# A zero-padded last token tile in the low-rank sums, and six small attention groups moved behind the second layer of an older batch's small group

## The chip, the cores and the metric

The kernel runs on one core of a Trainium2 chip. The metric is device time in microseconds (us) of one execution. PE is TensorE, DVE is VectorE, ACT is ScalarE, POOL is GpSimd, and SP is SyncE, which issues all the transfers of this kernel.

## The reference

There are eight batches of 3136 tokens with 256 features. A gated attention is followed by a mixer with a low-rank sum over tokens and a two-layer network over features:

```
attn = maximum(z @ z.T / 3136, 0) ** 2      # z is 3136 x 64
x    = u * (attn @ v)                       # u, v are 3136 x 256
u2   = x + ((x.T @ U) @ V).T                # U is 3136 x 32, V is 32 x 3136
out  = u2 + maximum(u2 @ w_ch1, 0) @ w_ch2  # 256 -> 1024 -> 256
```

Inputs and output are float32; the matmuls work on bf16 copies.

## The kernel before, in words

The tokens of a batch are 25 tiles of 128 rows: 24 full ones and a last one with 64 rows (TAIL). Four full tiles make a group, so a batch has six groups of 512 tokens (g = 0 to 5) and a small group of 64 tokens (g = 6, called NQ). An item is one group of one batch; the kernel walks through 56 items (b, g), in order, and at each item it mixes work of three stages: the attention of (b, g); u2 of the group one batch earlier; and the two layers of the network (ch1 and ch2) for the group one batch and one item earlier. In item (b, 0) the last of these is the small group of batch b-2.

The order on every engine is written by the program itself. A planner keeps a clock in units of 256 matmul columns, an estimate of when ACT, DVE and SP come free (`book`, L109), and when each of the four PSUM buffers comes free (`ps_free`, `take_ps`). `emit` (L971) walks through a list of light units, which are pairs of matmuls of the attention sum or of ch2, and slips other work in at given places; an entry of such a queue is (place, PSUM buffers that must be free, urgent or not, function), and a place that needs buffers waits up to 14 units for them. Work for ACT and DVE that is not due yet is put into `held`. Each engine then does its instructions in that order.

Most matmuls are pairs: each operand is split into two halves of 64 rows, and the two halves are run side by side in tile shape 64*128 (rows * columns of TensorE). Both halves add into the same PSUM banks at different times; where they change banks, `post` (L164) puts a no-op on POOL that waits for the last matmuls on the old banks, and the next matmul waits for that no-op (recorded at L168 in the profile). A stream such as `ch2_stream` (L908) goes through all its units with one crossing of halves and banks, calls `post`, and then through all of them with the other: two passes of 16 pairs.

The names that the change and the steps of the prediction touch:

- `load_u` (L291) loads u of a group. All groups share the tile u_sb with two buffers.
- `score_small` makes the scores of the small group, one item before the batch begins. `last_turn` has the DMA transpose them for the full groups.
- `av_small` (L654) multiplies them with v: 50 matmuls of shape 64*64, whose four partial sums are added by `four_sums` (an ACT copy at L680, DVE adds at L682 and L684) and multiplied with u at L672. It runs in item (b, 6), the last of its batch, as `small` (L1289). Where that item has a ch2 stream, it is put at half of it, between the two passes: `qm += [(nC // 2, -1, False, small)]`. Items 6 and 55, the first and the last of these, have no such stream.
- `t1_all` (L737) makes the low-rank sum over all tokens of a batch at place 8 of the next batch's item 0: 24 matmuls of shape 128*32 and one of 64*32, for the last tile.
- `u2_unit` (L768) makes u2 of a group, casts it and has the DMA transpose it to u2T (`x_turn`, L730) for ch1. The first group's is marked as urgent; its ch1 begins at place 4 of item (b, 1).
- `ch2_small` (L951) is the second layer of a small group: 16 matmuls of shape 64*64 and `four_sums`. It runs in item (b, 0) of the second batch after its own: `qc.append((72, 1, False, lambda: ch2_small(*fin)))`.
- `issue_turn` (L371) has the DMA transpose a block of scores into the mirrored one (L384), or part of a diagonal block (L376).

All transfers stand in one queue on SP, in the order in which the program issues them; one that waits holds those behind it.

Of the kernel before, what the change touches and what calls it, by code (L numbers as in the profile page):

```python
# [8 lines left out]
FP32 = mybir.dt.float32  # L9
BF16 = mybir.dt.bfloat16  # L10
# [8 lines left out]
def kernel(  # L19
# [11 lines left out]
    nc = tc.nc  # L31

    B, S, D = u.shape
# [3 lines left out]
    P = 128  # L37
    NT = (S + P - 1) // P
    NF = S // P
# [4 lines left out]
    GT = 4  # L44
# [245 lines left out]

    def load_u(b, g):  # L291
        g0, gw = groups[g]
        t = pool.tile([P, GT, D], FP32, name="u_sb", bufs=2)
        if gw >= P:
            nc.sync.dma_start(
                out=t[:, : gw // P, :],
                in_=rows_of(u[b])[:, g0 // P : (g0 + gw) // P, :],
            )
        else:
            nc.sync.dma_start(out=t[:gw, 0, :], in_=u[b, g0 : g0 + gw, :])  # L300
        queued(gw)
        u_sbs[b, g] = t
# [292 lines left out]
    def av_stream(b, g, box):  # L595
        def lhs(h, q, jt):
            jb, j = divmod(jt, GT)
            while (b, jb) not in v_cast:
                if spare and not b:
                    spare.pop(0)()  # L600
                else:
                    run_held(min(h[0] for h in held))
            while (b, g, jb) not in blocks:
                if (g, jb, b) in ready_turns:
                    issue_turn((g, jb, b))
                else:
                    run_held(min(h[0] for h in held))
            t = blocks[b, g, jb][1]
            if jb >= g or made_twice(b, g, jb):
                while squared.get((b, g, jb), 0) < 2:  # L610
                    run_held(min(h[0] for h in held))
                if split(b, g, jb):
                    while j >= 2 and q < 2 and (b, g) not in split_turned:
                        if (g, g, b) in ready_turns:
                            issue_turn((g, g, b))
                        else:
                            run_held(min(h[0] for h in held))
                    x = in_split(j, q)
                    return t.rearrange("p a c -> p (a c)")[h, x : x + P]
                return t[h, j, q * P : (q + 1) * P]  # L620

            return t.rearrange("p a c -> p (a c)")[h, (q * GT + j) * P : (q * GT + j + 1) * P]

        per = 2 * GT

        def step(i, way, first, least):
            if first:
                xs[b, g] = pool.tile([P, GT, D], BF16, name="x_bf", bufs=8)
                box["k"], box["ps"] = take_ps()
            jt, a = divmod(i, 2)  # L630
            pair(
                box["k"],
                crossed(
                    way,
                    a,
                    lambda h, q: dict(
                        out=four(box["ps"])[:, q, :],
                        lhsT=lhs(h, q, jt),
                        rhs=v_bfs[b][h, jt, :],
                        start=first,  # L640
                        stop=False,
                    ),
                ),
                D,
            )
            while box.get("given", 0) < least // per:
                give_block(blocks[b, g, box.get("given", 0)])
                box["given"] = box.get("given", 0) + 1

        return Ways(2 * NF, 1, step, box)  # L650

    def av_small(b, g):  # L654
        k, ps = take_ps()
        rows = groups[g][1]
        xs[b, g] = pool.tile([P, GT, D], BF16, name="x_bf", bufs=8)
        for jt in range(NT):
            c = jt % 2
            for h in range(2):  # L660
                nc.tensor.matmul(  # L661
                    out=ps[c * hp : c * hp + rows, h, :D],
                    lhsT=smalls[b][h * hp : (h + 1) * hp, place_of(jt), :],
                    rhs=v_bfs[b][h * hp : (h + 1) * hp, jt, :],
                    start=(jt < 2),
                    stop=(jt >= NT - 2),
                    tile_position=(h * hp, c * hp),
                )
        pe(NT / 2 + 2)
        u1 = u_sbs[b, g]  # L670
        four_sums(k, ps, u1[:rows, 1:3, :])
        nc.vector.tensor_tensor(  # L672
            out=xs[b, g][:rows, 0, :], in0=u1[:rows, 1, :], in1=u1[:rows, 0, :], op=ALU.mult
        )
        book("dve", clock[0] + 3, 3)
# [61 lines left out]
    def t1_all(b):  # L737
        k, pt = take_ps()
        for g in range(NG):
            for q, it, rows in tiles_of(g):  # L740
                c = it % NREP
                nc.tensor.matmul(  # L742
                    out=pt[c * R : (c + 1) * R, 0, :D],
                    lhsT=U_bf[:rows, it, :],
                    rhs=xs[b, g][:rows, q, :],
                    start=(it < NREP),
                    stop=(it + NREP >= NT),
                    tile_position=(0, c * R),
                )
        pe(8)  # L750

        up = pool.tile([P, D], FP32, name="t1_up", bufs=1)
        t1 = pool.tile([P, D], BF16, name="t1_sb")
        nc.scalar.copy(out=up[:hp, :], in_=pt[hp:, 0, :D])
        nc.vector.tensor_tensor(out=t1[:hp, :], in0=pt[:hp, 0, :D], in1=up[:hp, :], op=ALU.add)
        nc.vector.tensor_copy(out=t1[hp:, :], in_=t1[:hp, :])
        book("act", clock[0] + 3, 5)
        ps_free[k] = book("dve", clock[0] + 10, 6)
        t1s[b] = t1
# [270 lines left out]
    def load_U():  # L1030
        entry, raw = stage_block()
        nc.sync.dma_start(out=raw[:, : NF * R].rearrange("p (t r) -> p t r", r=R), in_=rows_of(moe_U))
        nc.sync.dma_start(out=raw[:TAIL, NF * R : NT * R], in_=moe_U[NF * P :, :])
        queued(NF * R / 2)

        def casts():
            cast(U_bf[:, :NF, :], raw[:, : NF * R].rearrange("p (t r) -> p t r", r=R), NF * R)
            cast(U_bf[:TAIL, NF, :], raw[:TAIL, NF * R : NT * R], 100)
            give_block(entry)

        return [casts]
# [158 lines left out]
        todo[t] = todo[t][:most]  # L1200

    direct = (B - 1, 0)
    for t in range(n_items):
        slot[0] = t
        att = items[t]
# [4 lines left out]
        g_now = t % NG  # L1210
        b_next = t // NG + 1

        if t + 1 < n_items and t > NG:
            load_u(*items[t + 1])
        if t == n_items - 3:
            xTs[direct] = take_block()[1][:, : GT // 2, :].rearrange("p a (q d c) -> p (a q) d c", d=ND, c=P)
            x_turn(*direct, xTs[direct])
# [46 lines left out]
        if av and full:  # L1264

            last = nA - 9
            for h, x, y in zip(hs, (4, 22, 36, 62), (16, 32, 48, last)):
                qc.append((x, 1, False, one(h, 0)))
                qc.append((y, 0 if y == 32 else 1, y != 32, lambda h=h, y=y: (scores(y != 32), one(h, 1)())))
            n = len(mine) - 3  # L1270
            qs += [(9 + 74 * i / n, 1, False, lambda: scores(1)) for i in range(n)]
        elif av:

            for h, x in zip(hs, (22, 32, 42, 52)):
                qc += [(x, 1, False, one(h, 0)), (x + 8, 0, False, one(h, 1))]
            if fin:
                qc.append((72, 1, False, lambda: ch2_small(*fin)))
            k = min(2, len(mine) // 3)
            n = len(mine) - 3 * k
            at = [1 + 80 * i / n for i in range(n)]  # L1280
            if t == 0:
                at = [8, 8, 26, 38, 42, 56, 64, 72, 80]
                for i, x in ((2, 22), (3, 34)):
                    qm.append((x, 0, False, lambda i=i: z_turn(0, i * 2 * GT, on_act)))
            qs += [(x, 1, False, lambda: scores(1)) for x in at]
            qs += [(x, k, True, lambda: scores(k)) for x in (16, 48 if t else 46, nA - 2) if k]
        else:

            small = lambda: av_small(*att)  # L1289
            order = mine[:1] + [small] + mine[1:]  # L1290
            if mix:
                c0, c1, d0, d1, c2, c3, d2, d3 = parts(mix, box1)
                up = [lambda: u2_unit(*u2i)]
                if fin:
                    order = [c0] + mine[:1] + [c1, d0, d1] + [c2] + mine[1:] + [c3, d2, d3] + up
                else:
                    order = up + [small, c0, c1, d0, d1, c2, c3, lambda: t1_all(att[0]), d2, d3]
            qc += [(0, 0, False, f) for f in order]
# [79 lines left out]
```

## Time and profile before

| what | value |
|---|---|
| median of 3 runs | 992.4 us (991.75 to 994.2) |
| the profiled execution | 994.29 us, with a span of 992.5 us |
| PE, weight loads, DVE, ACT, POOL busy | 98%, 79%, 62%, 50%, 2% |
| granted TensorE clock | 1.00 |
| DMA | 176.4 MB, queue q1 86.8% of 16 engines' span |
| start of one small attention group to the next, batches 1 to 6 | 120.10 us, once 120.56 |
| PE waiting for another engine | 13.3 us in all, 7.3 of it for the first z tiles |

A row of the view of groups has the line, engine, operation and tiles, the shape and count, then busy time and mean length of one, then the idle time before them and what ended it. The view in order of time has start, length, engine, line, operation and tiles; neighbouring records of one kind are merged (x50). Ends of matmuls are modelled, so lengths of matmuls overlap; starts are recorded. "SPq" is SP issuing a transfer: its length is that of the issue, and the landing is told apart.

### The profile page before, as it was taken

Reading aid. Unit: us, or ns where it says so; the run is one execution under the profiler, and the core shown is the slowest. Engines: PE = TensorE matmul, PEld = TensorE weight load, DVE = VectorE, ACT = ScalarE, POOL = GpSimd, SP = SyncE. Lnnn points to the kernel's source line nnn. Section 1 sums busy time; section 2 is a strip of 40 time slices with the busy share of each in tenths; the row PEclk is TensorE's granted clock in tenths of the full one; section 3 lists DMA queues with packets and bytes.
Section 4 is the critical chain, followed back from the end, with each engine's and each line's share of the span. In section 5 each row is a group of like instructions: output and inputs, shape, how many; then the busy total and the mean of one; then the engine's idle time right before and its main releaser. Section 6 shows DMA issues by size and latency. Waiting matters only on the chain.

```text
span 992.5 us, 35366 instructions
## 1 busy us (share of the span) xinstructions
PE 973.9 (98%) x16137; PEld 781.0 (79%) x16137; DVE 618.2 (62%) x793; ACT 491.4 (50%) x584; POOL 17.3 (2%) x24
## 2 busy tenths in 40 slices
PE   6999999999999999999999999999999999999997
PEld 3898788877778777787778877788777877787776
DVE  5977765668556675566756667555765666643453
ACT  5887742457324573355533465434653256422353
POOL 4100000000000000000000000000000000000000
PEclk9999999999999999999999999999999999999999
DMA  7999999889997799787998799975999889964142
GB/s 246 192 213 226 199 205 213 196 145 216 211 181 165 168 215 203 198 139 180 215 213 173 131 192 211 209 169 130 206 230 189 150 170 168 166 123 103 46 110 91
DMA packets 371974, 176.38 MB, mean 178 GB/s; under 512 B 347248, under 2 KB 350320, under 8 KB 371824
## 3 DMA queue, kind: packets, MB, share of 16 engines
q1 hardware_dynamic: 371824, 174.12, 86.8%
q8 instruction: 126, 2.06, 0.9%
q14 instruction: 24, 0.20, 0.1%
HBM read 62.56 MB, written 25.69 MB: 89 GB/s over the span
## 4 chain that ended last, share of the span: by engine, by line
PE 96%; DMA 1%; DVE 1%; ACT 1%; issue 0%; POOL 0%; SPq 0%; POOLq 0%; ACTq 0%
PE ps L178 93%; PE ps L661 1%; PE ps L742 1%; DMA blk<-in_v_dram 1%; DVE blk L348 1%; DMA u2T<-x_bf 0%; ACT blk L358 0%; PE ps L957 0%; ACT blk L906 0%; POOL z_bf L229 0%; DVE blk L354 0%; DVE blk L943 0%; DVE x_bf L694 0%; POOL v_bf L249 0%; PE ps L315 0%
## 5 line engine op out<-in xcount | busy, mean ns | idle before, releaser
L178 PEld LDWEIGHTS <-blk 64*128 64x128 bf16 x12288 | 617.2, 94 | 149.0 <-POOLq L168 7.7
L178 PE MATMUL ps<-v_bf,blk 64*128 64x256 bf16 x9216 | 612.6, 269 | 3.6 <-DVE blk L348 1.8
L358 ACT ACTIVATE blk<-ps 128x1024 bf16<-128x1024 f32 x339 | 319.6, 974 | 365.6 <-PE ps L178 354.2
L348 DVE TENSOR_TENSOR blk<-blk 128x1024 bf16<-128x1024 bf16 x352 | 226.4, 666 | 42.7 <-ACT blk L358 42.1
L178 PE MATMUL ps<-u2T,w_bf 64*128 64x512 bf16 (+1 forms) x1792 | 236.9, 349 | 0.5 <-DMA u2T<-x_bf 0.3
L178 PE MATMUL ps<-w_bf,blk 64*128 64x256 bf16 x3072 | 193.7, 269 | 0.2
L903 DVE TENSOR_SCALAR blk<-ps 128x1024 bf16<-128x1024 f32 (+1 forms) x110 | 127.1, 1155 | 92.9 <-PE ps L178 92.9
L906 ACT ACTIVATE blk<-ps 128x1024 bf16<-128x1024 f32 (+1 forms) x114 | 97.7, 866 | 91.6 <-PE ps L178 91.2
L178 PE MATMUL ps<-zzT 64*128 64x512 bf16 (+2 forms) x902 | 130.2, 329 | 1.7 <-ACT zzT L324 1.7
L178 PEld LDWEIGHTS <-w_bf 64*128 64x128 bf16 x1792 | 90.5, 94 | 29.2 <-POOLq L168 4.1
L694 DVE TENSOR_TENSOR x_bf<-ps,u_sb 128x1024 bf16<-128x1024 f32 x48 | 58.7, 1224 | 70.7 <-PE ps L178 70.7
L815 DVE TENSOR_TENSOR out_sb<-ps,x_bf 128x1024 f32<-128x1024 f32 (+1 forms) x49 | 54.2, 1107 | 59.3 <-PE ps L178 59.3
L943 DVE TENSOR_TENSOR out_sb<-ps,out_sb 128x1024 f32<-128x1024 f32 x42 | 51.3, 1222 | 18.3 <-PE ps L178 18.3
L178 PEld LDWEIGHTS <-zzT 64*128 64x128 bf16 x902 | 41.8, 95 | 8.0 <-ACT zzT L324 2.2
L178 PE MATMUL ps<-t_sb,V_bf 64*128 64x256 bf16 x200 | 20.8, 269 | 0.0
L198 ACT CAST x_bf<-out_sb 128x1024 bf16<-128x1024 f32 (+1 forms) x21 | 17.3, 826 | 6.0 <-DVE out_sb L815 6.0
L200 DVE CAST v_bf<-stage 128x1024 bf16<-128x1024 f32 (+1 forms) x33 | 20.2, 611 | 0.0
L178 PE MATMUL ps<-v_bf,last_sb 64*128 64x256 bf16 x192 | 18.6, 269 | 0.0
L354 DVE TENSOR_SCALAR blk<-ps 128x1024 bf16<-128x1024 f32 (+1 forms) x9 | 10.0, 1106 | 12.9 <-PE ps L178 12.9
L943 DVE TENSOR_TENSOR blk<-ps,blk 128x1024 f32<-128x1024 f32 x6 | 7.3, 1225 | 16.0 <-PE ps L178 15.9
L682 DVE TENSOR_TENSOR u_sb<-ps,u_sb 64x512 f32<-64x512 f32 x8 | 5.5, 682 | 17.1 <-ACT u_sb L680 17.1
L198 ACT CAST v_bf<-stage 128x1024 bf16<-128x1024 f32 x15 | 15.6, 1040 | 0.0
(67 smaller groups left out, 227.7 us busy)
## 6 DMA issues: line engine op xcount, KB each, us to landing
u_sb<-in_u_dram SPq DMA_DIRECT2D x48, 512.0 KB, 5.3
stage<-in_v_dram SPq DMA_DIRECT2D x42, 512.0 KB, 6.2
out_dram<-out_sb SPq DMA_DIRECT2D x42, 512.0 KB, 3.1
stage<-in_z_dram SPq DMA_DIRECT2D x7, 512.0 KB, 6.0
blk<-in_v_dram SPq DMA_DIRECT2D x6, 512.0 KB, 7.1
out_dram<-blk SPq DMA_DIRECT2D x6, 512.0 KB, 2.6
blk<-blk SPq DMA_TRANSPOSE x156, 5.2
blk<-in_moe_w_ch_dram SPq DMA_DIRECT2D x4, 512.0 KB, 5.5
```

Of the source, the lines that this page charges most:

```text
L178: ins = nc.tensor.matmul(**args)
L198: nc.scalar.copy(out=out, in_=in_)
L200: nc.vector.tensor_copy(out=out, in_=in_)
L348: nc.vector.tensor_tensor(out=a, in0=a, in1=a, op=ALU.mult)
L354: nc.vector.tensor_scalar(out=dst, in0=src, scalar1=scale, scalar2=0.0, op0=ALU.mult, op1=ALU.max)
L358: nc.scalar.activation(out=dst, in_=src, func=AF.Relu, scale=scale)
L661: nc.tensor.matmul(out=ps[c * hp : c * hp + rows, h, :D], lhsT=smalls[b][h * hp : (h + 1) * hp, place_of(jt), :], rhs=v_bfs[b][h * hp : (h ...
L694: nc.vector.tensor_tensor(out=xs[b, g][:rows, :n, :], in0=four(box["ps"])[:rows, :n, :], in1=u_sbs[b, g][:rows, :n, :], op=ALU.mult,)
L815: nc.vector.tensor_tensor(out=o[:rows, :n, :], in0=four(ps)[:rows, :n, :], in1=x, op=ALU.add)
L903: nc.vector.tensor_single_scalar(out=r, in_=ps[:, :, :gw], scalar=0.0, op=ALU.max)
L906: nc.scalar.activation(out=r, in_=ps[:, :, :gw], func=AF.Relu)
L943: nc.vector.tensor_tensor(out=o, in0=acc, in1=o, op=ALU.add)
```

## The change

Four edits go together.

- The multiplied x of a small group gets a tile of its own (x_small, two buffers), whose rows 64 to 127 are set to zero; U's last tile gets zeros in the same rows, and `t1_all` uses all 128 rows for every tile. x_bf goes from 8 buffers to 7.
- u of a small group gets a tile of its own (u_small, one buffer).
- For batches 2 to 7 (`early`), `av_small` leaves item (b, 6) and is called right behind `ch2_small` of batch b-2 in item (b, 0), an entry that now asks for two free PSUM buffers. Batches 0 and 1 keep their place.
- From item (1, 6) on, u of the next batch's small group is loaded at the start of item (b, 6), behind that of the next batch's first group.

```diff
--- before.py
+++ after.py
@@ -290,13 +290,14 @@
 
     def load_u(b, g):
         g0, gw = groups[g]
-        t = pool.tile([P, GT, D], FP32, name="u_sb", bufs=2)
         if gw >= P:
+            t = pool.tile([P, GT, D], FP32, name="u_sb", bufs=2)
             nc.sync.dma_start(
                 out=t[:, : gw // P, :],
                 in_=rows_of(u[b])[:, g0 // P : (g0 + gw) // P, :],
             )
         else:
+            t = pool.tile([P, 3, D], FP32, name="u_small", bufs=1)
             nc.sync.dma_start(out=t[:gw, 0, :], in_=u[b, g0 : g0 + gw, :])
         queued(gw)
         u_sbs[b, g] = t
@@ -625,7 +626,7 @@
 
         def step(i, way, first, least):
             if first:
-                xs[b, g] = pool.tile([P, GT, D], BF16, name="x_bf", bufs=8)
+                xs[b, g] = pool.tile([P, GT, D], BF16, name="x_bf", bufs=7)
                 box["k"], box["ps"] = take_ps()
             jt, a = divmod(i, 2)
             pair(
@@ -654,7 +655,11 @@
     def av_small(b, g):
         k, ps = take_ps()
         rows = groups[g][1]
-        xs[b, g] = pool.tile([P, GT, D], BF16, name="x_bf", bufs=8)
+        xs[b, g] = pool.tile([P, 1, D], BF16, name="x_small")
+        nc.vector.memset(xs[b, g][rows:, 0, :], 0.0)
+        for jt in range(NQ + 1):
+            while (b, jt) not in v_cast:
+                run_held(min(h[0] for h in held))
         for jt in range(NT):
             c = jt % 2
             for h in range(2):
@@ -741,8 +746,8 @@
                 c = it % NREP
                 nc.tensor.matmul(
                     out=pt[c * R : (c + 1) * R, 0, :D],
-                    lhsT=U_bf[:rows, it, :],
-                    rhs=xs[b, g][:rows, q, :],
+                    lhsT=U_bf[:, it, :],
+                    rhs=xs[b, g][:, q, :],
                     start=(it < NREP),
                     stop=(it + NREP >= NT),
                     tile_position=(0, c * R),
@@ -1035,6 +1040,7 @@
 
         def casts():
             cast(U_bf[:, :NF, :], raw[:, : NF * R].rearrange("p (t r) -> p t r", r=R), NF * R)
+            nc.vector.memset(U_bf[TAIL:, NF, :], 0.0)
             cast(U_bf[:TAIL, NF, :], raw[:TAIL, NF * R : NT * R], 100)
             give_block(entry)
 
@@ -1200,6 +1206,10 @@
         todo[t] = todo[t][:most]
 
     direct = (B - 1, 0)
+
+    def early(b, g):
+        return b > 1 and g == NQ
+
     for t in range(n_items):
         slot[0] = t
         att = items[t]
@@ -1210,8 +1220,10 @@
         g_now = t % NG
         b_next = t // NG + 1
 
-        if t + 1 < n_items and t > NG:
+        if t + 1 < n_items and t > NG and not early(*items[t + 1]):
             load_u(*items[t + 1])
+        if t > NG and g_now == NQ and b_next < B:
+            load_u(b_next, NQ)
         if t == n_items - 3:
             xTs[direct] = take_block()[1][:, : GT // 2, :].rearrange("p a (q d c) -> p (a q) d c", d=ND, c=P)
             x_turn(*direct, xTs[direct])
@@ -1274,7 +1286,7 @@
             for h, x in zip(hs, (22, 32, 42, 52)):
                 qc += [(x, 1, False, one(h, 0)), (x + 8, 0, False, one(h, 1))]
             if fin:
-                qc.append((72, 1, False, lambda: ch2_small(*fin)))
+                qc.append((72, 2, False, lambda: (ch2_small(*fin), av_small(att[0], NQ))))
             k = min(2, len(mine) // 3)
             n = len(mine) - 3 * k
             at = [1 + 80 * i / n for i in range(n)]
@@ -1286,7 +1298,7 @@
             qs += [(x, k, True, lambda: scores(k)) for x in (16, 48 if t else 46, nA - 2) if k]
         else:
 
-            small = lambda: av_small(*att)
+            small = (lambda: None) if early(*att) else (lambda: av_small(*att))
             order = mine[:1] + [small] + mine[1:]
             if mix:
                 c0, c1, d0, d1, c2, c3, d2, d3 = parts(mix, box1)
```

## The prediction

> **What bounds the kernel now.** I read the page first, then the windows view cut at the starts of the eight small attention groups, then the order-of-time view of TensorE (PE), SyncE (SP) and VectorE (DVE) around one of them. The page says that PE is busy for 98% of the span, that the chain that ended last is 96% PE, and that two kinds of PE work wait in front of a sequencer (the last columns of its weight-load row):
>
> ```profile
> PE 973.9 (98%) x16137; PEld 781.0 (79%) x16137; DVE 618.2 (62%) x793; ACT 491.4 (50%) x584; POOL 17.3 (2%) x24
> PE 96%; DMA 1%; DVE 1%; ACT 1%; issue 0%; POOL 0%; SPq 0%; POOLq 0%; ACTq 0%
> L178 PEld LDWEIGHTS <-blk 64*128 64x128 bf16 x12288 | 617.2, 94 | 149.0 <-POOLq L168 7.7
> ```
>
> So time is PE time: what shortens PE's instruction stream, or makes PE wait, counts in full; work of DVE or ScalarE (ACT) counts only where PE stands for it. A batch is a fixed length, and the one that is longer has one late transfer:
>
> ```profile
> 217.19:337.29 120.10, 120.10 (x2012) 96.06 (x2010) 76.35 (x98) 57.21 (x70) 0.00 (x0) 1.00 0.95 186
> 577.49:698.05 120.56, 120.27 (x2013) 96.06 (x2011) 76.35 (x98) 57.21 (x70) 0.00 (x0) 1.00 0.93 185
> ```
>
> The columns are the window, its length, the busy time of PE, weight loads, DVE, ACT and POOL, then the granted clock (full), the DMA share (0.95, to be kept in mind) and GB/s. The 0.46 us more of the second window is PE waiting at 596.86 for the transposed u2T.
>
> **The change part by part.**
>
> *A. The last token tile with 128 rows (all 8 batches).* In the single records, two 64*128 matmuls (the row halves) start within 19 ns of each other and the next pair 90 ns later. Where the tile shape changes, the next start comes 199 to 203 ns after the last one, and 211 ns at the way out of 64*32. A t1 burst has three such changes: in to 128*32, to 64*32 for its last matmul, out. With 128 rows the middle one goes: 203 + 211 becomes about 100 (a new group of four) + 203, so 0.11 us less, times 8: **-0.89 us**. The two zero fills are DVE work with one cover, the PE bound: the one new fill per batch stands ahead of work that waits for PE anyway.
>
> *B. The small attention group behind ch2_small (batches 2 to 7).* PE now, in the order-of-time view:
>
> ```profile
> 215.16 0.27 PE L178 MATMUL ps<-t_sb,V_bf 64*128 64x256 bf16 x1
> 215.26 2.00 PE L178 MATMUL ps<-w_bf,blk 64*128 64x256 bf16 x31
> 217.19 1.61 PE L661 MATMUL ps<-v_bf,attn_small 64*64 64x256 bf16 x50
> 218.73 0.50 PE L178 MATMUL ps<-w_bf,blk 64*128 64x256 bf16 x6
> ...
> 224.73 0.22 PE L178 MATMUL ps<-u2T,w_bf 64*128 64x64 bf16 x4
> ```
>
> The 50 matmuls (1.54 us) stay; they only move. They and the 16 of ch2_small have the same shape, so one way out (201) and one way in (199) go, and a plain step of about 100 and one of 90 take their places: 0.21 us, times 6: **-1.26 us**.
>
> *C. What the small group covered.* It stands exactly between the two passes of the second layer's stream (16 pairs, 50 small matmuls, 16 pairs above). At that turn `post` puts a no-op on GpSimd that waits for the last matmul of the first pass, and the second pass waits for the no-op. Now 1.54 us of other work lies between. In the changed program's instruction order nothing does, in the five items that end batches 2 to 6 (batch 7's has no such stream). Such a bare turn is in the trace near the end:
>
> ```profile
> 938.96 1.11 PE L178 MATMUL ps<-w_bf,blk 64*128 64x256 bf16 x12
> 939.90 0.22 PE L178 MATMUL ps<-u2T,w_bf 64*128 64x64 bf16 x4
> ```
>
> Twelve such matmuls need 12 x 54.5 = 654 ns, and 940 pass: 0.29 us lost (one record-to-record step is 384 ns in place of 90; the turn at 985.3 shows 383). Turns with 382 ns of work between show no loss, and with 273 ns lose 66. So 5 x 0.294: **+1.47 us**. This gives back the whole of B.
>
> *D. The new load of u.* The diff gives the small group's u a single buffer and loads batch b+1's at the start of item (b, 6). From batch 2 on the small group has then long been done. At the end of batch 1 it has not: its small group stays in that item, so the load waits there for the last multiply of av_small (L672). SP issues in order; behind the load stand, in the program's order, a block transpose (L384), the small group's u2T transpose (L730), a store, the next u, z and its tails. Before:
>
> ```profile
> 213.35 0.42 SPq L295 DMA_DIRECT2D u_sb<-in_u_dram  x1
> 215.52 3.85 SPq L384 DMA_TRANSPOSE blk<-blk  x1
> 219.46 1.20 SPq L730 DMA_TRANSPOSE u2T<-x_bf  x1
> 222.20 0.34 SPq L945 DMA_DIRECT2D out_dram<-out_sb  x1
> ```
>
> ```profile
> 220.62 0.42 DVE L672 TENSOR_TENSOR x_bf<-u_sb 64x256 bf16<-64x256 f32 x1
> ```
>
> The u2T landed 4.0 us after its issue, at 223.5, and PE first needs it at 224.73 (row above): 1.3 us of cover. After: L672 ends at 221.04 - 0.11 (A, once); the load takes 0.4 to issue, L384 1.7 to 3.9 (1.66 and 1.94 where nothing was ahead of it, 3.85 here), u2T starts at about 223.3 and lands 3.3 later, at 226.6 (the seven small ones: 3.1 to 4.0, the very first 7.3). PE needs it at 224.73 - 0.2 = 224.5. PE stands 2.1 us, once. Ends: 1.7 (1.66 and 3.1) and 4.9 (3.85 and 4.0). I take the short L384, since SP and the queues have run empty by then: **+2.1 us**. The transfers behind it come some 3 us late, but PE's need for them is later by the same stall and by the 1.5 us of the moved group: last_sb lands near 235 for a need at 238.7, the next u2T near 237.4 for 239.
>
> [...]
>
> *E. Around the moved group.* Its u2_unit-to-ch1 distance: the next u2T of a batch's first group gains 1.5 us of cover, since the small group now lies between its issue and its use; the stall at 596.86 goes: **-0.4 us**. In items (b, 6) the small u2T loses cover: PE's way from u2_unit to its use is 1.4 us shorter, and the cover was 2.8, 2.1, 1.9, 3.0 and 2.5 us in those batches; 0.5 remains at the least, so I cost it at nothing; a landing 1 us later would cost up to 0.5 in some of five. In items (b, 0) the planner's order shifts: one PSUM buffer is asked for again 504 ns of PE work after its last matmul, with a 0.3 us ACT pass (the 128x128 rows of L906) between. Such a buffer came free 0.57 us after the block's start (225.88, ACT 226.15 to 226.45), and the block is 55 ns: 5 x 0.02, **+0.1 us**; 0.3 each if ACT is behind. The two small sums now stand one behind the other on DVE and hold it about 2 us longer than one; PE asks for those PSUM buffers 2.9 and 3.4 us after, the chain (ACT 0.58, DVE 0.68) needs 1.4. Cost nothing; up to 0.5 x 6 if squares queue behind.
>
> **Sum**: -0.89 - 1.26 + 1.47 + 2.1 - 0.4 + 0.1 = **+1.1 us**. The profiled execution took 994.29 us (span 992.5), so it would be 995.4; against the median, 992.4, it is **993.5**. What cannot be told from no change in this kernel is about 0.3%, 3.0 us.
>
> **The rivals.**
> 1. *The stall of D is hidden*: the wait is over sooner, or the transposes land faster than their rows. Against it: 221.04 is later than the 219.46 at which u2T is issued now, by more than its cover. Then C against A and B remain: -1.0 us, **991.4**. Chance 0.12.
> 2. *C is hidden too*, by other work that slides into the turn: -0.89 - 1.26 - 0.4 = -2.5, **989.9**, and with luck past the 0.3%. Against it: the order has none there. Chance 0.06.
> 3. *Slower: the standstill of SP costs more than one wait.* With DMA at 0.95, L384 takes its 3.85 again and u2T lands as late as the 7.3 us of the first small one: 221.45 + 3.85 + 0.1 + 7.3 = 232.7, a stall of 8.2 us, sum +7.2, **999.6**. It decides from a stall of 4.0 us on (the rest is -1.0, and 3.0 are needed). The lost cover of E works the same way, five times. For it: the DMA share. Against it: the engines drain while SP stands. Chance 0.18.
> 4. The forecast, within +-3 us: 0.64.
>
> **Numbers.** Faster by over 0.3% 0.05 (half of rival 2 and a little), within 0.3% 0.77 (forecast, rival 1, the rest of 2), slower 0.18. The range leaves out rival 2 and the upper part of 3: 991.0 (rival 1, less 0.4) to 996.9 (D at 4.9 with some of E's bounds).
>
> **What would show it.** A: t1 bursts with no 64*32 form and one change less. B: ch2_small and the small group in one stretch; with A, 8 + 12 = 20 changes of shape fewer. C: five steps near 384 ns in the second layer's stream at the ends of batches 2 to 6, and more than 7.7 us at POOLq. D: an SP gap from 214 to 221 and one PE wait for u2T near 224.5. E: no wait at 596. A batch in the middle should be near 120.10 - 0.11 - 0.21 + 0.29 = 120.07. If that batch is longer by half a microsecond, E is wrong; if PE does not stand near 224.5, D is.

## The result and the profile after

The change takes 995.46 us (median of 14 runs) and the kernel before, in the same comparison, 993.13 us: a ratio of 1.0023, with a 95% interval of 1.0015 to 1.0031. That is +2.3 us where +1.1 was forecast. The time forecast was 993.5 us, added up from a median of three runs that lies 0.7 us lower than the one here; the result is inside the range of 991.0 to 996.9, and the difference is inside what was called no change. A second comparison, further down, gave 1.0013 (1.0003 to 1.0023). The profiled execution after took 994.14 us, span 992.4; before, 994.29 and 992.5.

The two spans seem equal, but their first 97 us are not: the first small group starts at 97.62 us before and at 96.44 after, since the start-up waits for z differ from one execution to the next (95.6 to 98.5 us over the nine traces). From there to the last `ch2_small` it is 885.45 us before and 886.48 after: +1.03 us. Traces are compared over this stretch from here on; "the stretch" below always means it.

These lines of the page answer to those of before. They are the busy shares, the chain, and the weight loads whose wait for the no-op on POOL grew from 7.7 to 9.7 us.

```profile
PE 973.1 (98%) x16137; PEld 785.3 (79%) x16137; DVE 624.6 (63%) x807; ACT 487.9 (49%) x579; POOL 17.2 (2%) x24
PE 96%; ACT 1%; DVE 1%; DMA 1%; issue 0%; POOLq 0%; ACTq 0%
L178 PEld LDWEIGHTS <-blk 64*128 64x128 bf16 x12288 | 620.0, 94 | 150.0 <-POOLq L168 9.7
```

This is the windows view after, cut at the starts of the low-rank sums of batches 1 to 4. The columns are as in the prediction:

```profile
220.43:342.48 122.05, 120.11 (x2011) 96.07 (x2010) 76.92 (x100) 57.32 (x70) 0.00 (x0) 1.00 0.92 186
342.48:462.58 120.10, 119.99 (x2012) 96.71 (x2010) 77.51 (x101) 56.48 (x69) 0.00 (x0) 1.00 0.91 184
462.58:582.68 120.10, 119.99 (x2012) 96.78 (x2011) 77.51 (x101) 56.49 (x69) 0.00 (x0) 1.00 0.98 188
```

A batch in the middle is as long as before, 120.10 us, and the first of these windows is 1.95 us longer: that is D, once. The batch near 596, which had the 0.46 us of a late u2T, is 120.10 now. These rows show PE, then SP, then VectorE at the place of D, each in order of time:

```profile
223.27 0.27 PE L178 MATMUL ps<-v_bf,blk 64*128 64x256 bf16 x2
225.37 0.23 PE L178 MATMUL ps<-u2T,w_bf 64*128 64x64 bf16 x4 [1.83 <-DMA u2T<-x_small]
```

```profile
219.83 0.48 SPq L301 DMA_DIRECT2D u_small<-in_u_dram  x1
220.40 1.77 SPq L385 DMA_TRANSPOSE blk<-blk  x1
222.26 1.90 SPq L735 DMA_TRANSPOSE u2T<-x_small  x1
```

```profile
219.38 0.42 DVE L677 TENSOR_TENSOR x_small<-u_small 64x256 bf16<-64x256 f32 x1
```

SP issues the load 30 ns after the multiply ends at 219.80, then the block transpose, then the u2T that PE needs. SP's transfer before the load was issued at 212.10, so SP stood for 7.2 us. The u2T lands 3.1 us after its issue, at 225.36, and PE starts at 225.37.

The moved group of batch 3, in order of time on PE:

```profile
352.58 0.63 PE L962 MATMUL ps<-w_bf,blk 64*64 64x256 bf16 x16
353.04 1.58 PE L666 MATMUL ps<-v_bf,attn_small 64*64 64x256 bf16 x50
354.56 0.61 PE L178 MATMUL ps<-v_bf,blk 64*128 64x256 bf16 x8
```

It follows `ch2_small` with a plain step of 100 ns. In the single records the turn of the second layer's stream, now bare, has a step of 383 to 384 ns at 339.2, 459.3, 579.4, 699.5 and 819.6 us, the five that were named. These are the no-op at the first of them and who waited for it (us, times):

```profile
L168 POOLq EVENT_SEMAPHORE  x1: 17/17/17, 339.5 to 339.5; - x1
  PEld L178: 0.4, 1
```

In the kernel before, the no-op of this turn at the end of batch 1 runs at 217.3, while the small group's matmuls are under way, and nobody waits for it.

### The profile page after: what moved, and what is told of

It reads as the page before. It is cut to its first block, busy times and chain, and to the rows that moved or that the text cites. A ratio compares the mean times of both kernels' runs of the same rounds, so it can differ in the third digit from the quotient of the medians.

```text
span 992.4 us, 35375 instructions
## 1 busy us (share of the span) xinstructions
PE 973.1 (98%) x16137; PEld 785.3 (79%) x16137; DVE 624.6 (63%) x807; ACT 487.9 (49%) x579; POOL 17.2 (2%) x24
## 4 chain that ended last, share of the span: by engine, by line
PE 96%; ACT 1%; DVE 1%; DMA 1%; issue 0%; POOLq 0%; ACTq 0%
PE ps L178 94%; PE ps L666 1%; PE ps L747 1%; DVE blk L349 1%; PE ps L962 0%; ACT blk L359 0%; DMA u2T<-x_small 0%; ACT blk L911 0%; ACT blk L1165 0%; DMA blk<-in_z_dram 0%; PE ps L316 0%; DVE blk L355 0%; DVE blk L948 0%; DVE x_bf L699 0%; ACT zzT L325 0%
## 5 line engine op out<-in xcount | busy, mean ns | idle before, releaser
L359 ACT ACTIVATE blk<-ps 128x1024 bf16<-128x1024 f32 (+1 forms) x334 | 315.0, 973 | 366.6 <-PE ps L178 358.2
L908 DVE TENSOR_SCALAR blk<-ps 128x1024 bf16<-128x1024 f32 (+1 forms) x110 | 127.2, 1156 | 92.3 <-PE ps L178 91.8
L911 ACT ACTIVATE blk<-ps 128x1024 bf16<-128x1024 f32 (+1 forms) x114 | 97.5, 865 | 102.2 <-PE ps L178 101.7
L820 DVE TENSOR_TENSOR out_sb<-ps,x_bf 128x1024 f32<-128x1024 f32 x42 | 51.4, 1224 | 61.3 <-PE ps L178 60.0
L355 DVE TENSOR_SCALAR blk<-ps 128x1024 bf16<-128x1024 f32 (+1 forms) x14 | 16.1, 1149 | 12.9 <-PE ps L178 12.9
L200 DVE CAST x_bf<-out_sb 128x1024 bf16<-128x1024 f32 x21 | 14.5, 689 | 0.3
L198 ACT CAST x_bf<-out_sb 128x1024 bf16<-128x1024 f32 x14 | 14.5, 1037 | 0.0
```

The source lines that it names most:

```text
L198: nc.scalar.copy(out=out, in_=in_)
L200: nc.vector.tensor_copy(out=out, in_=in_)
L355: nc.vector.tensor_scalar(out=dst, in0=src, scalar1=scale, scalar2=0.0, op0=ALU.mult, op1=ALU.max)
L359: nc.scalar.activation(out=dst, in_=src, func=AF.Relu, scale=scale)
L820: nc.vector.tensor_tensor(out=o[:rows, :n, :], in0=four(ps)[:rows, :n, :], in1=x, op=ALU.add)
L908: nc.vector.tensor_single_scalar(out=r, in_=ps[:, :, :gw], scalar=0.0, op=ALU.max)
```

## The experiments

The theory is the five terms A to E of the prediction. The rivals were that SP's standstill costs nothing or more than that, that the turn costs nothing, and that padding pays for itself with other costs. All kernels ran in five rounds beside the kernel before. Code is shown in extracts; `...` stands for lines left out.

**Without the wait on SP** (e1_no_sp_wait). The change, but the small groups of batches 0 and 1 keep their u in u_sb:

```diff
-        if gw >= P:
+        if gw >= P or b < 2:
             t = pool.tile([P, GT, D], FP32, name="u_sb", bufs=2)
+        else:
+            t = pool.tile([P, 3, D], FP32, name="u_small", bufs=1)
...
```

> The change without its wait on SP: u of the small groups of batches 0 and 1 stays in u_sb, so that the first load into u_small (batch 2) waits for nothing. Theory (the prediction's terms A to E): the 2.0 us of D go and the rest stays, -0.9 - 1.3 + 1.5 - 0.4 = about -1 us against the kernel before (ratio 0.999), no PE wait for u2T near 224, and five steps of 383 ns remain. The medians show 1.2 us more than the sum. If that is D being longer in other executions than in the profiled one, this kernel comes out at -1; if it is the cover that the small u2T lost in items (b, 6), it comes out near 0 to +0.3 (ratio 1.000). Rival (the standstill of SP is not what costs): no gain against the change, ratio 1.002.

Measured: 993.61 against 993.96 us, ratio 0.9997 (0.9988 to 1.0006). In the trace the stretch is 884.26 us, 1.2 less than before and 2.2 less than with the change; PE no longer waits for u2T anywhere, and the five steps of 384 to 385 ns are there. SP, in order of time, does not stand at the load any more, and u2T is issued at 219.63, in the kernel before at 219.46:

```profile
213.95 0.79 SPq L303 DMA_DIRECT2D u_small<-in_u_dram  x1
215.65 3.89 SPq L387 DMA_TRANSPOSE blk<-blk  x1
219.63 1.18 SPq L737 DMA_TRANSPOSE u2T<-x_small  x1
```

D is this wait. Whether what the medians show beyond the sum belongs to it, the interval (-1.2 to +0.6 us) does not tell.

**The padding alone** (e2_pad_only), on the kernel before:

```diff
-        xs[b, g] = pool.tile([P, GT, D], BF16, name="x_bf", bufs=8)
+        xs[b, g] = pool.tile([P, 1, D], BF16, name="x_small")
+        nc.vector.memset(xs[b, g][rows:, 0, :], 0.0)
...
-                    lhsT=U_bf[:rows, it, :],
-                    rhs=xs[b, g][:rows, q, :],
+                    lhsT=U_bf[:, it, :],
+                    rhs=xs[b, g][:, q, :],
...
+            nc.vector.memset(U_bf[TAIL:, NF, :], 0.0)
```

> Part A alone, on the kernel before: x_small with zeros, U's zeros, 128 rows in every matmul of the low-rank sum. Theory: 8 changes of tile shape fewer at 0.11 us, -0.9 us, ratio 0.9991; PE shows no 64*32 form. Rival (the zero fills or the fuller tile cost as much as the shape change): ratio 1.000 or above.

Measured: 993.1 against 993.96, ratio 0.9983 (0.9975 to 0.9992). A batch takes 119.99 us in the windows view, 0.11 less, in every batch:

```profile
222.27:342.26 119.99, 119.99 (x2021) 96.08 (x2013) 76.52 (x100) 57.19 (x71) 0.00 (x0) 1.00 0.93 185
```

In the stretch this execution is 1.5 us shorter than the profiled one of before: 0.89 of A, 0.46 of a u2T that was late there and is not here, and some 0.2 of other steps. A is confirmed in size by the batches. The runs are in line with it: -0.9 us by the difference of the medians, -1.7 by the ratio, and the interval (-2.5 to -0.8 us) holds A's -0.89.

**The low-rank sum in the turn** (e3_t1_at_turn). In the change, the small group of a batch is done early, so the sum over the batch's tokens can be made in item (b, 6), in place of the small group that stood in the turn:

```diff
         if not av:
-            qm += [(nC // 2, -1, False, small)] if nC else []
+            turn = (lambda: t1_all(att[0])) if early(*att) else small
+            qm += [(nC // 2, -1, False, turn)] if nC else []
...
-            if u2i[1] == 0:
+            if u2i[1] == 0 and not early(u2i[0], NQ):
                 qm.append((8, 1, False, lambda: t1_all(u2i[0])))
```

> The change, with the low-rank sum of batches 2 to 6 moved into the bare turn between the two passes of the second layer's stream in item (b, 6), which the earlier small group makes possible. Theory: the no-op on POOL is covered again, C goes, 1.5 us less than the change: ratio 1.0008 by the medians; no steps of 383 ns at the ends of batches 2 to 6; the stall of 2.0 us near 224 stays. Rival (the turn is not what costs, or the low-rank sum waits for the last x of the batch there): no gain, ratio 1.002 or more, with PE waiting in front of the low-rank sum.

Measured: 994.53 against 993.96, ratio 1.0004 (0.9994 to 1.0015). No step of 383 ns is left at the ends of batches 2 to 6, and a batch takes 119.78 us: 120.10 - 0.11 - 0.21, that is A and B without C. The stall of D is there, 2.02 us in this execution. Its stretch, 886.94 us, is not shorter than the change's, although five turns are covered. Most of the reason is in the windows view around D:

```profile
224.57:227.98 3.41, 1.39 (x29) 0.91 (x26) 1.48 (x3) 1.82 (x2) 0.00 (x0) 1.00 0.95 241
227.98:231.39 3.41, 3.41 (x44) 2.39 (x40) 2.52 (x3) 0.55 (x2) 0.00 (x0) 0.50 0.98 299
231.39:234.81 3.42, 3.42 (x70) 2.79 (x68) 1.49 (x3) 3.09 (x5) 0.00 (x0) 1.00 1.16 200
```

For the 3.41 us that begin 0.95 us after the stall, the granted TensorE clock is 0.50, and pairs of 256 columns start 213 ns apart in place of 109. That costs 1.7 us; the stall is 0.2 longer than in the change, and a step near 154 us is 0.1 longer. Together they outweigh the 1.6 us that the covered turns save. Neither profiled execution of the change has such a drop.

**Both** (e4_both): the two edits above together.

> Both of the above: no wait on SP, and the low-rank sum in the turn. Theory: A + B + E are left, -0.9 - 1.3 - 0.4 = -2.5 us against the kernel before, ratio 0.9975, so it beats both. If the 1.2 us that the medians show beyond the sum belong to the lost cover of the small u2T, -1.3 us, ratio 0.9987. Rival: the two removals do not add, ratio 1.000.

Measured: 990.97 against 993.96, ratio 0.9967 (0.9954 to 0.998). The stretch is 882.76 us: 2.7 less than before, 3.7 less than the change, and 1.50 less than e1_no_sp_wait, from which this kernel differs in the turn alone. None of these four traces has a drop of the clock within the stretch. The turn of batch 2 in order of time, 16 pairs, the low-rank sum, 16 pairs:

```profile
336.68 2.01 PE L178 MATMUL ps<-w_bf,blk 64*128 64x256 bf16 x31
338.62 0.84 PE L749 MATMUL ps<-x_bf,U_bf 128*32 128x256 bf16 x24
339.28 0.27 PE L749 MATMUL ps<-x_small,U_bf 128*32 128x256 bf16 x1
339.49 1.92 PE L178 MATMUL ps<-w_bf,blk 64*128 64x256 bf16 x32
```

The sum covers the no-op with 0.87 us of work; the page's wait for it is back to 7.6 us, from 9.7 in e1_no_sp_wait. This version beats both kernels, the one before by 0.3%.

**SP's wait six times** (e5_sp_wait_six_times): the kernel before with A, and u of the small groups loaded early into the one buffer u_small, while these groups stay in item (b, 6), so that every load waits for the group of its own item.

```diff
...
-        if t + 1 < n_items and t > NG:
+        if t + 1 < n_items and t > NG and not (g_now == NQ - 1 and b_next > 2):
             load_u(*items[t + 1])
+        if t > NG and g_now == NQ and b_next < B:
+            load_u(b_next, NQ)
```

> The kernel before with A, a single u_small buffer and the early load of u, but with the small groups left in item (b, 6): the load now waits for the small group of its own item at the end of batches 1 to 6, six times in place of once. Theory (the wait holds SP's queue, and the small u2T behind it comes 2.0 us too late): -0.9 + 6 x 2.0 = +11 us against the kernel before, ratio 1.011, with a PE wait for the small u2T of some 2 us in each of six batches. Rival (the stall of batch 1 was the catching-up of a busy DMA start-up phase, and later batches have the cover, 1.9 to 3.0 us there): less than +4 us, with waits well under 1 us in the later batches.

Measured: 1013.66 against 993.44, ratio 1.0202 (1.0185 to 1.0219): +20 us, where the theory had +11 and the rival less than +4. These are the two longest rows of the waits view of PE, and from that of SP the row of the load (us in total, times, longest):

```profile
PE ps L178 <- DMA u2T<-x_small: 13.0, 6, 3.0
PE ps L178 <- DMA u2T<-x_bf: 4.2, 4, 2.0
```

```profile
SPq L301 <- DVE x_small L674: 43.3, 6, 7.2
```

SP stands 7.2 us each time; the small u2T is late six times, by 1.7 to 3.0 us and 2.2 on the average, 13.0 us where the theory had 12. The rest was not expected. In four of the batches the next transposed u2T, that of the first group, is late too, by 0.3 to 2.0 us, and last_sb once. In the change it is not; the moved group then lies before its use, which fits, but was not tested apart. And after two of the six stalls the clock is halved again:

```profile
719.73:723.14 3.41, 3.41 (x44) 2.40 (x42) 2.52 (x3) 0.57 (x3) 0.00 (x0) 0.50 0.98 321
842.61:849.43 6.82, 5.97 (x70) 4.18 (x72) 2.52 (x3) 0.97 (x3) 0.00 (x0) 0.50 1.06 214
```

Against e2_pad_only, which has A and no early load, the stretch is 24.1 us longer (908.05 and 883.94). By the steps of the single records, the six small u2T account for 14.0 of it and the five later transfers for 5.4. The two batches with a drop are 4.6 us longer than their stalls explain, which is the work done at half the clock. The sum is 24.0.

**The turn laid bare six times** (e6_turn_bare_six_times), on the kernel before:

```diff
-            qm += [(nC // 2, -1, False, small)] if nC else []
+            qm += [(nC, -1, False, small)] if nC else []
```

> The kernel before, but the small group stands behind the whole second-layer stream of its item and not between its two passes, in the six items that have one; nothing else moves. Theory (C): six bare turns at 0.29 us, +1.8 us, ratio 1.0018, with six steps of 383 ns. Rival (the turn costs nothing, since PE's lead elsewhere absorbs it): ratio 1.000, and no such steps or batches of 120.10 us all the same.

Measured: 997.92 against 993.44, ratio 1.005 (1.0036 to 1.0063): +4.5 us by the medians, not 1.8. The six steps of 383 to 384 ns are there, at 216.1 and so on. But the edit moves something else. The low-rank sum now begins 1.2 us after PE's first matmul behind the small group (340.64 to 341.84), before it was 2.9 us (218.73 to 221.67), and the sum's last matmul waits for its x (order of time):

```profile
339.11 1.61 PE L661 MATMUL ps<-v_bf,attn_small 64*64 64x256 bf16 x50
...
341.84 0.84 PE L742 MATMUL ps<-x_bf,U_bf 128*32 128x256 bf16 x24
343.01 0.27 PE L742 MATMUL ps<-x_bf,U_bf 64*32 64x256 bf16 x1 [0.33 <-DVE x_bf L672]
```

That step is 605 ns in place of 203. 0.29 + 0.40 = 0.69 us, and a batch is 120.78 us, 0.68 more than 120.10. Six of them are 4.1 us; the stretch, 888.90 us, is 3.4 longer than the one before, which has a late u2T of 0.46 that is not here. C's size is confirmed by the step; the expectation had overlooked the second wait.

**The change again** (e7_change_again), beside the last two.

> The change itself once more, beside these two, for a second trace of it and more runs. Theory: the sum of A to E, +1.0 us from the first small group to the last second layer as in its first trace; by the medians +1 to +2.3 us, ratio 1.001 to 1.0023. If the ratio stays at 1.0023 or above and the trace shows D at 2.0 us again, some 1 us of the difference is not in the terms A to E.

Measured: 994.3 against 993.44, ratio 1.0013 (1.0003 to 1.0023). The stretch is 886.32 us, +0.87; PE waits 1.80 us for the small u2T before 227.2, and the batches after it are 120.10 again.

## Why the prediction was right

- **A**, -0.89 forecast: 0.11 us in every batch of e2_pad_only.
- **B**, -1.26 forecast: 119.99 (A alone) to 119.78 (A and B, turn covered) is 0.21 in a batch. The steps at the changes of tile shape in batches 1 to 6 of the change's trace are 199 to 205 ns, against 99 to 100 between `ch2_small` and the small group.
- **C**, +1.47 forecast: five steps of 383 to 384 ns in both traces of the change, none where the low-rank sum stands in the turn, and 1.50 us between e1_no_sp_wait and e4_both.
- **D**, +2.1 forecast: PE waits 1.83 and 1.80 us in the two traces of the change, and the batch is 1.95 and 1.92 us longer (122.05 and 122.02); nothing of it without the wait. The path was right too: the block transpose took the short 1.77 us, and u2T landed 3.1 us after its issue. What D leaves out is what followed the stall of 2.02 us in e3_t1_at_turn: 3.41 us at a granted clock of 0.50, some 1.7 us more. Behind the stalls in the two profiled executions of the change there was no such drop (see the last section).
- **E**, -0.4 and +0.1 forecast: no late u2T at the first group's ch1 in either trace of the change. Whether that is the cover gained is only partly shown: e1_no_sp_wait has none either, but neither has e2_pad_only, which has no such cover; e5_sp_wait_six_times shows that the place is short of cover when SP is late. The batch of 120.10 us is 0.03 more than A + B + C make of it (120.07); the small term was forecast at 0.02 a batch and may be this, but no run shows where it lies.
- The cover that the small u2T loses in items (b, 6) was costed at nothing, and no wait for it appears after the one of D.
- **The sum**, +1.1: +1.03 and +0.87 us by the stretch of two traces. By the ratios of the runs it is +2.3 and +1.3 us. The first interval begins at 1.0015, 1.5 us, so by it some half a microsecond or more is not in these terms; the second begins at 1.0003 and asks for nothing more. What it is stays open. The profiled executions are single ones, and what lies outside the stretch takes 105.0 to 107.9 us in the nine traces. The clock does not explain it: two of the 26 runs of the change (996.5 and 996.63 us) show a granted clock of 0.998, which would fit one drop of 1.7 us, and the other 24 show 0.999 or 1.000, like the runs of the kernel before that stood beside the experiments. Two runs do not move the medians.

Rivals 1 and 2 (a hidden stall, a hidden turn) are out by the rows above. Rival 3 did not come in the change, but a part of it is real: in e5_sp_wait_six_times the standstill went on to the next transfers, and in two kernels the granted clock fell to 0.50 behind it.

## What to carry to other kernels

Before work is moved away, look at what it stood between: the small group covered a way through another engine's no-op that costs 0.29 us where it is bare, and moving it gave back more than the two saved changes of tile shape brought (1.47 us against 1.26), until another 0.87 us of work was put there. The single buffer that is refilled early turned into a wait of the issuing queue at the one place where its old user was still to come (7.2 us of SP), and the price was paid at the transfers behind it (1.83 us of PE). Where start-up times vary by more than the change is worth, compare a stretch between two fixed points of the traces, and look at the granted clock by windows within it: a mean of 0.997 over an execution hid the 1.7 us that decided one comparison here.

## What was not expected of the hardware

In e5_sp_wait_six_times a standstill of SP of 7.2 us cost PE 1.7 to 3.0 us at the first late transfer and, in four of six batches, 0.3 to 2.0 us more at one issued some ten microseconds later. There a queue that had fallen behind had not caught up over the issues that lay between, ten of them at the end of batch 2.

Three times in the nine traces the granted TensorE clock fell to 0.50 within the stretch, each time behind a stall of PE: in e3_t1_at_turn for 3.41 us, which begin 0.95 us after the stall of 2.02 us, and in e5_sp_wait_six_times for 3.41 and 6.82 us, behind two of the six stalls for the small u2T (1.7 to 3.0 us). Behind the other four of them there was no drop, nor behind the stalls of 1.83 and 1.80 us in the two traces of the change. What sets the clock, and why these stalls differ, no run shows.
